# Weight subtractions and additions of a mixture-of-experts stage from GpSimd to VectorE, PSUM copies to ScalarE

## The chip, the cores and the metric

The kernel runs on one core of one Trainium2 chip. The metric is the device time of one execution in microseconds, as the median of several runs. TensorE multiplies, VectorE, ScalarE and GpSimd work on elements, SyncE's queue issues nearly all DMA transfers.

## The reference

Linear attention (random features) with a mixture of experts and a feed-forward behind it:

```python
q_p, k_p = (phi(q_s), phi(k_s))
...
x = np.ascontiguousarray(attn_out.transpose(0, 2, 1, 3)).reshape(B * S, H * D)
...
for e in range(E):            # E = 8, D = 512, F = 1024
    mask = expert_idx == e
    ...
    h = np.maximum(xe @ w1[e], 0.0)
    ye = h @ w2[e]
    out[mask] = gate_w[mask, None] * ye
...
h = x @ w_in                                            # 2304 x 512 times 512 x 2048
g = np.maximum(h, 0.0) + np.log1p(np.exp(-np.abs(h)))
return (g @ w_out).astype(np.float32)
```

The experts' weights are float32; w_in and w_out come as 64-bit floats.

## The kernel before

The program has three stages: attention with routing, the eight experts one after the other, and the feed-forward over 6 blocks of 384 tokens. Every product is made of three matmuls on operands that are split into a rounded part and a rest (`three`, L881 to L884), so each weight is first copied to a rounded form by ScalarE, and the rest is found by a subtraction.

An expert (`moe_expert`, L946) has 8 steps f. A step has 12 matmuls of the first layer into a bank "a", then ScalarE's relu hh (L957) and VectorE's rest hl (L958), and 12 matmuls of the second layer (`layer2`, L934) for the step two behind. Two banks hold "a", so TensorE comes back to the bank of step f, and to its hh and hl, only after the second layer's 12 matmuls, the next step's 12 and again 12 of the second layer.

Weights come through four buffers "raw" of 512 KB. `fetch_unit` (L251) issues the DMA on SyncE's queue; in the next step `split_unit` (L257) rounds the unit on ScalarE (L260) and subtracts (L263), on GpSimd for odd units and on VectorE for even ones. Each expert brings in 8 units, 64 in the stage, so 32 subtractions are on either engine. In every third step, until all 16 are done, half a block of w_in is fetched too, in the same buffers; `convert_w_in` (L229) makes a float32 of it with four VectorE instructions (`split_f64`, L193 to L199), an addition on GpSimd (L231), and a store to the scratch tensor wi_f, issued by SyncE (L232). From the last expert on, halves of w_out are split by `load_half` (L217: VectorE, ScalarE, and GpSimd at L222 and L223).

The next expert's x is gathered by GpSimd (L895), scaled by ScalarE (L906) and, part by part, transposed on TensorE (L913), rounded by ScalarE (L915) and its rest taken by VectorE (xl, L916). Behind an expert's last product `store_y` (L975) copies four PSUM banks to ys, two on VectorE (L981) and two on ScalarE (L983), and SyncE stores ys (L986) and the tokens' numbers (L989). `load_y` (L996) reads a block for the feed-forward, its rests by VectorE (L1005).

Each engine and SyncE's queue take their instructions in order; the order of the queues is planned when the program is built, from the program's order and a timeline of its own.

Of the kernel before, what the change touches and what calls it, by code (L numbers as in the profile page):

```python
# [15 lines left out]
AF = mybir.ActivationFunctionType  # L16
ALU = mybir.AluOpType
# [4 lines left out]
P = 128  # L22
# slots per expert: the first expert's, then the others' from the fullest to the emptiest
CAPS = (344, 344, 328, 312, 304, 292, 284, 264)
CAP = max(CAPS)
# [4 lines left out]
def tile_favor_moe_softplus(  # L30
# [42 lines left out]

    # a token's x and its gate
    x_tok = dram.tile([NT + P, DM + 1], F32, name="x_tok")
# [74 lines left out]
    def disjoint(ins, group):  # L150
        """Scatters of a group write rows of their own: none waits for another."""
        ins = getattr(ins, "ins", ins)
        tc.declare_no_dep(ins, group=group, reason="each token has a row of its own")
        tc.add_to_no_dep_group(group, ins)

    def behind(ins, other):
        """Of two instructions of an engine, the order."""
        if other is not None:
            tc.add_manual_dep(
                ins.ins, other.ins.name,  # L160
                mybir.DependencyInfo(mybir.DependencyClass.NoSync, mybir.DependencyReason.DATA),
                reason="keeps the engine's order")
# [3 lines left out]
    def expert_units(i, e):  # L166
        # the units of the expert at place i: expert e, a number or a register
        for j in range(4):
            a1 = w1[:, :, j * 256:(j + 1) * 256].rearrange("e (k p) f -> p e k f", p=P)
            a2 = w2[:, j * 256:(j + 1) * 256, :].rearrange("e (k p) f -> p e k f", p=P)  # L170
            units[8 * i + j] = a1[:, bass.ds(e, 1)].rearrange("p o k f -> p (o k) f")
            units[8 * i + 4 + j] = a2[:, bass.ds(e, 1)].rearrange("p o k f -> p (o k) f")
# [14 lines left out]
    def split_f64(raw, after):  # L187
        """64-bit floats as a float32 of their upper bits and a float32 of the rest."""
        hi, lo = raw[:, :, 1], raw[:, :, 0]
# [12 lines left out]

    # weights come a step or more before they are split: no engine waits for them

# [24 lines left out]
    def convert_w_in(j, hf, raw, after):  # L229
        a, _, r = split_f64(raw, after)  # L230
        nc.gpsimd.tensor_tensor(r, a, r, op=ALU.add)  # L231
        nc.sync.dma_start(units[8 * E + j][:, 2 * hf:2 * hf + 2, :],  # L232
                          r.rearrange("p (k f) -> p k f", k=2))
# [23 lines left out]
    def split_unit(i, raw, after):  # L257
        slot = ring[i % NRING]
        for c in range(0, 1024, 1024):
            ins = nc.scalar.activation(slot[:, c:c + 1024], raw[:, c:c + 1024], AF.Copy)  # L260
            if c == 0:
                behind(ins, after[0])
            (nc.gpsimd if i % 2 else nc.vector).tensor_tensor(  # L263
                slot[:, 1024 + c:1024 + c + 1024], raw[:, c:c + 1024],
# [4 lines left out]

# [1 line left out]
    pctx = ExitStack()  # L271
# [11 lines left out]
    with ExitStack() as actx:  # L283
# [5 lines left out]
        nc.gpsimd.memset(zero_w, 0.0)  # L289
        # NT: no token  # L290
        none_i = sm.tile([P, E * NT // P], I32, name="none_i", bufs=1)
# [7 lines left out]
        def clear_y():  # L299
            # rows that the first gather meets before their tokens' are written, or for no token  # L300
            nc.sync.dma_start(x_tok[NT:NT + P, :], zero_w)
# [9 lines left out]
            for c in range(KD):  # L311
                for j in range(0, NT, 512):
# [5 lines left out]
                       allow_small_or_imprecise_dtypes=True)  # L318
        # a token's number less NT, in two parts
        tok_hl = sm.tile([P, NTILE, 2], I32, name="tok_hl", bufs=1)  # L320
# [73 lines left out]

        # An item: the token tiles r, r+1 (or the mixed one) of a batch pair, of k or of q.
        class Item:
# [12 lines left out]
        xin, vin = {}, {}  # L409
        # the last items' tokens reach the first expert without a way through DRAM  # L410
        tail = items[-2:]
# [19 lines left out]
        def half_squares(it):  # L431
            it.sq = sm.tile([P, H, it.nr], F32, tag="sq", bufs=2, name="sq")
            step = 4 if it is items[0] else H
            for h in range(0, H, step):
                nc.vector.tensor_reduce(it.sq[:, h:h + step], it.x2[:, h:h + step], axis=AX.X,
                                        op=ALU.add)
            # sq cancels in (proj - sq) - (max - sq): (sq - ln(sqrt(M))) - sq
            up = sm.tile([P, H, it.nr], F32, tag="up", bufs=2, name="up")
# [7 lines left out]
        def transposes(it, g4):  # L446
# [8 lines left out]
            if it is items[1] and g4 == 0:  # L455
                behind(ins, first_done[0])
            # in a slot of the ring that is free so far
            k0 = DM * (1 + lows[0] % 3)
# [45 lines left out]

        # heads per bank; a head's two products with its neighbours' zeros overlap there
        GROUPS = ((0, 3), (3, 6), (6, 8))
# [25 lines left out]

        # kv per head: gate columns, z and kv of the first batch, then kv, z, gate of the second
        kvs = {}
# [30 lines left out]

        # where the 128 columns of a product start in kv, and where g, z and x are in a product;
        # the next product overwrites the columns that are not needed
        KV0 = (0, 2 * DG - P)
# [14 lines left out]
        def q_product(it, grp):  # L583
# [18 lines left out]
            def cols(g, lo, hi, c0, w):  # L602
                # [p, head, tile, w]: the columns c0, c0 + 1, ... of each product
                a = nm[lo:hi, c0:c0 + w]
# [25 lines left out]
        def route_pick(it):  # L630
# [17 lines left out]
            nc.vector.tensor_tensor(it.oh, cand, bc(cm), op=ALU.is_equal)  # L648
            # the one-hots before each tile of the item, summed
            it.ohs = sm.tile([P, 2, E], BF16, tag="ohsum", name="ohsum")  # L650
# [31 lines left out]
        def read_first():  # L682
            """The tokens of the first window so far."""
            nc.sync.dma_start(ids_0, id_slot[0:NC * P, :].rearrange("(c p) o -> p (c o)", p=P))

        def add_first(it, sl):
            """An item's tokens in the first window, by one-hots of their slots."""
            pid = ps.tile([P, NC, 2], F32, tag=TG, bufs=NTG, name="pid")
# [13 lines left out]
        def gather_first():  # L702
            """The rows of the first window, but for those of the last items."""
            for c in range(NC):
# [4 lines left out]
        def first_split():  # L709
            """The first window's x, transposed: gathered rows, and one-hots for the last items'."""  # L710
            xh, xl = (ring[i][:, 0:KD * NBLK].rearrange("p (k n) -> p k n", k=KD)
# [75 lines left out]
        NI = len(items)  # L787
        # the first expert's weights come when the second pair's k leaves time
        UNITS_AT = {10: (0, 1), 11: (2, 3), 12: (4, 5), 13: (6, 7)}
# [7 lines left out]
        for n in range(NI + 2):  # L797
# [47 lines left out]
            if n == NI - 2:  # L845
                # in the space of k and v
                a, b = (inp.tile([P, VO], F32, tag="kf", bufs=2, name="tail") for _ in range(2))
# [31 lines left out]

# [1 line left out]
    def three(o, wH, wL, xH, xL, first, last):  # L881
# [46 lines left out]

    # products of the second layer that are due, LAG steps behind the first layer's
    due = []  # L930
# [15 lines left out]
    def moe_expert(e, xh, xl, mid):  # L946
        n_e = CAPS[e]
        for f in range(NF):
# [17 lines left out]
            if f % 3 == 1 and to_convert:  # L966
                fetch_w_in(*to_convert.pop(0))
            # the first expert's x stays in the slots of units 11 and 15 until its last use
            for j in ((0, 4, 1, 5, 2, 6, 3, 7)[f:f + 1] if e or f < 6 else (3, 7) if f == 7 else ()):
# [5 lines left out]
    def store_y(e):  # L975
# [3 lines left out]
        for d in range(KD):  # L979
            if d % 2:  # L980
                nc.vector.tensor_copy(ys[:, d, 0:n_e], ops[d][:, 0:n_e])  # L981
            else:
                nc.scalar.activation(ys[:, d, 0:n_e], ops[d][:, 0:n_e], AF.Copy)  # L983
        reg = nc.sync.value_load(off_i[0:1, e:e + 1], min_val=max(0, NT - sum(CAPS[e:])),
# [25 lines left out]
    def places():  # L1010
        # tokens per expert; the experts behind the first by their tokens, the fullest first
        key = tb.tile([P, E], F32, tag="over", name="key")
# [21 lines left out]
        nc.vector.tensor_reduce(cntp[:, 1:E], more, axis=AX.X, op=ALU.add)  # L1034
        # where the places' windows start in the compact order
        off = tb.tile([P, E + 1], F32, tag="off", name="off")
# [13 lines left out]
    def windows():  # L1050
        # overflow windows: 128 slots each of the experts that hold more tokens than their slots
        over = tb.tile([P, E], F32, tag="over", name="over")
# [43 lines left out]

    # the parts of the next expert's x that are transposed in a step
    SPLIT_AT = {2: (0,), 3: (1,), 4: (2,), 5: (3,)}
# [29 lines left out]

# [1 line left out]
    def ff_layer1(a, f, yh, yl):  # L1130
# [54 lines left out]
    def ff_step(b, f, gh, gl):  # L1185
        if b == NB - 1 and f >= NF2 - 2:
            # the last two steps tile by tile: the first tiles leave while the last is computed
            ends.append((f, gh, gl))
# [34 lines left out]

# [1 line left out]
    n_over = nc.values_load(ntot[0:1, 0:1], min_val=0, max_val=NWIN)  # L1225
# [87 lines left out]
```

## Time and profile before

| what | us |
|---|---|
| median of 3 runs | 923.97 |
| shortest, longest run | 920.7, 926.7 |
| profiled execution, span from first to last instruction | 919.6 |

The page gives no time for the profiled execution beside its span; the shortest of the runs shown is 1.1 us above the span, the median 4.4. In the rows, a busy time is a sum over instructions in us, "mean" and the durations of a source view are in ns, and "idle before" is the time that the engine stood just before those instructions, with what ended it. PEclk is the granted TensorE clock as a share of full speed. A wait in SyncE's queue (SPq) delays all DMAs behind it.

### The profile page before, as it was taken

Reading aid. Unit: us, or ns where it says so; the run is one execution under the profiler, and the core shown is the slowest. Engines: PE = TensorE matmul, PEld = TensorE weight load, DVE = VectorE, ACT = ScalarE, POOL = GpSimd, SP = SyncE. Lnnn points to the kernel's source line nnn. Section 1 sums busy time; section 2 is a strip of 40 time slices with the busy share of each in tenths; the row PEclk is TensorE's granted clock in tenths of the full one; section 3 lists DMA queues with packets and bytes.
Section 4 is the critical chain, followed back from the end, with each engine's and each line's share of the span. In section 5 each row is a group of like instructions: output and inputs, shape, how many; then the busy total and the mean of one; then the engine's idle time right before and its main releaser. Section 6 shows DMA issues by size and latency. Waiting matters only on the chain.

```text
span 919.6 us, 14049 instructions
## 1 busy us (share of the span) xinstructions
PE 839.2 (91%) x5104; PEld 776.2 (84%) x5104; DVE 528.6 (57%) x1127; ACT 473.5 (51%) x1051; POOL 298.5 (32%) x290
## 2 busy tenths in 40 slices
PE   7798878995999899898997988999999999999996
PEld 6697778985899898798897976989898999999995
DVE  6489889985796685754688878323223323222221
ACT  4476658761544444444545545555545555445543
POOL 6454467422344544454355554100100100001001
PEclk9799998997989999998999999999999999999999
DMA  9992352024768668667675420101001000000001
GB/s 244 210 317 85 82 161 69 1 71 70 240 190 258 227 198 271 196 202 230 213 254 195 133 94 14 56 1 35 35 1 34 36 1 1 35 1 18 19 1 36
DMA packets 83308, 104.22 MB, mean 113 GB/s; under 512 B 16904, under 2 KB 62632, under 8 KB 83234
## 3 DMA queue, kind: packets, MB, share of 16 engines
q1 hardware_dynamic: 79442, 93.35, 33.8%
q0 software_dynamic: 3792, 9.92, 3.7%
q8 instruction: 42, 0.69, 0.4%
q14 instruction: 32, 0.26, 0.1%
HBM read 78.68 MB, written 24.58 MB: 112 GB/s over the span
## 4 chain that ended last, share of the span: by engine, by line
issue 40%; PE 19%; DVE 19%; DMA 12%; POOL 4%; ACT 3%; SPq 1%; POOLq 0%; DVEq 0%; ACTq 0%
DMA raw<-in_moe_w_dram 5%; DVE cva L193 2%; DVE w L263 2%; PE a L882 2%; PE a L884 2%; PE a L883 2%; DVE cva L196 2%; PE nm L593 2%; DVE mx L489 2%; POOL out_dram L1176 1%; DMA x_tok<-xt 1%; DMA vm<-in_v_dram 1%; ACT w L260 1%; DVE cvr L199 1%; PE y L882 1%
## 5 line engine op out<-in xcount | busy, mean ns | idle before, releaser
L1144 DVE SCALAR_TENSOR_TENSOR ab<-a,ab 128x384 f32<-128x384 f32 x96 | 53.4, 556 | 175.9 <-ACT ab L1143 167.2
L882 PE MATMUL a<-yh,w 128*128 128x384 f32 x384 | 131.0, 341 | 11.8 <-DVE ab L1144 11.8
L884 PE MATMUL a<-yh,w 128*128 128x384 f32 x384 | 130.2, 339 | 0.0
L883 PE MATMUL a<-yl,w 128*128 128x384 f32 x384 | 129.5, 337 | 0.0
L1176 POOL DMA_INDIRECT out_dram<-ob,idx x18 | 17.8, 989 | 323.9 <-ACT ob L1174 320.2
L1159 PE MATMUL o<-w,gh 128*128 128x512 f32 x288 | 114.7, 398 | 0.0
L1156 PE MATMUL o<-w,gh 128*128 128x512 f32 x288 | 114.0, 396 | 0.0
L1161 PE MATMUL o<-w,gl 128*128 128x512 f32 x288 | 113.7, 398 | 0.0
L1141 ACT ACTIVATE ab<-a 128x384 f32<-128x384 f32 x96 | 46.9, 489 | 107.9 <-PE a L884 107.8
L493 ACT ACTIVATE ph<-pj,nb 128x128 f32<-128x128 f32 x288 | 82.6, 393 | 31.6 <-DVE nb L491 22.3
L260 ACT ACTIVATE w<-raw 128x1024 fp32r<-128x1024 f32 x64 | 67.5, 1056 | 58.8 <-DMA raw<-in_moe_w_dram 53.4
L263 POOL TENSOR_TENSOR w<-raw,w 128x1024 fp32r<-128x1024 f32 x32 | 77.1, 2427 | 58.5 <-ACT w L260 58.4
L882 PEld LDWEIGHTS a<-yh,w 128*128 128x128 f32 x384 | 72.4, 189 | 19.3 <-DVE ab L1144 15.4
L1148 DVE TENSOR_TENSOR gl<-ab,gh 128x384 fp32r<-128x384 f32 x96 | 55.5, 578 | 50.5 <-ACT gh L1147 50.5
L882 PE MATMUL y<-hh,w 128*128 128x344 f32 (+6 forms) x256 | 79.1, 313 | 2.4 <-DVE ys L981 2.1
L1147 ACT ACTIVATE gh<-ab 128x384 fp32r<-128x384 f32 x96 | 50.4, 525 | 57.7 <-DVE ab L1144 57.7
L883 PE MATMUL y<-hl,w 128*128 128x344 f32 (+6 forms) x256 | 79.9, 313 | 0.0
L884 PE MATMUL y<-hh,w 128*128 128x344 f32 (+6 forms) x256 | 79.1, 311 | 0.0
L263 DVE TENSOR_TENSOR w<-raw,w 128x1024 fp32r<-128x1024 f32 x32 | 58.6, 1833 | 31.8 <-ACT w L260 31.7
L883 PEld LDWEIGHTS a<-yl,w 128*128 128x128 f32 x384 | 72.8, 189 | 3.9
L884 PEld LDWEIGHTS a<-yh,w 128*128 128x128 f32 x384 | 72.4, 189 | 0.0
L882 PE MATMUL a<-xh,w 128*128 128x344 f32 (+6 forms) x224 | 70.2, 313 | 2.0 <-DVE hl L958 2.0
(223 smaller groups left out, 2039.0 us busy)
## 6 DMA issues: line engine op xcount, KB each, us to landing
raw<-in_moe_w_dram SPq DMA_DIRECT2D x64, 512.0 KB
raw<-in_moe_w_in_dram SPq DMA_DIRECT2D x16, 512.0 KB
raw<-in_moe_w_out_dram SPq DMA_DIRECT2D x16, 512.0 KB
yb<-y_comp SPq DMA_DIRECT2D x6, 768.0 KB
x_tok<-xt SPq DMA_DIRECT2D x8, 513.0 KB
vf<-in_v_dram SPq DMA_DIRECT2D x4, 1024.0 KB
qf<-in_q_dram SPq DMA_DIRECT2D x4, 1024.0 KB
y_comp<-w SPq DMA_DIRECT2D x16, 256.0 KB
```

The costliest lines, as they stand in the source:

```text
L260: ins = nc.scalar.activation(slot[:, c:c + 1024], raw[:, c:c + 1024], AF.Copy)
L263: (nc.gpsimd if i % 2 else nc.vector).tensor_tensor(slot[:, 1024 + c:1024 + c + 1024], raw[:, c:c + 1024], slot[:, c:c + 1024].bitcast(F32 ...
L493: ins = nc.scalar.activation(dst[j], pj[:, j // 2, j % 2, :], AF.Exp, bias=nb[:, j // 2, j % 2:j % 2 + 1])
L882: nc.tensor.matmul(o, lhsT=wH, rhs=xH, start=first, stop=False)
L883: nc.tensor.matmul(o, lhsT=wH, rhs=xL, start=False, stop=False)
L884: nc.tensor.matmul(o, lhsT=wL, rhs=xH, start=False, stop=last)
L1144: nc.vector.scalar_tensor_tensor(ab, a, 0.0, ab, op0=ALU.max, op1=ALU.add)
L1147: placed[0] = nc.scalar.activation(gh, ab, AF.Copy)
L1148: placed[1] = nc.vector.tensor_tensor(gl, ab, gh.bitcast(F32), op=ALU.subtract)
L1156: ins = nc.tensor.matmul(os[t], lhsT=gh[:, s], rhs=u[:, c:c + DM], start=f == 0, stop=False)
L1159: nc.tensor.matmul(os[t], lhsT=gh[:, s], rhs=u[:, 1024 + c:1024 + c + DM], start=False, stop=False)
L1161: ins = nc.tensor.matmul(os[t], lhsT=gl[:, s], rhs=u[:, c:c + DM], start=False, stop=f == NF2 - 1)
```

## The change

The subtraction of every weight unit (L263) is on VectorE, for odd units too; the addition of w_in's two parts (L231) is on VectorE; all four copies of an expert's result out of PSUM are ScalarE's. GpSimd keeps the gathers and, for w_out, L222 and L223. The diff also takes comments out, which is left out here.

```diff
     def convert_w_in(j, hf, raw, after):
         a, _, r = split_f64(raw, after)
-        nc.gpsimd.tensor_tensor(r, a, r, op=ALU.add)
+        nc.vector.tensor_tensor(r, a, r, op=ALU.add)
         nc.sync.dma_start(units[8 * E + j][:, 2 * hf:2 * hf + 2, :],
                           r.rearrange("p (k f) -> p k f", k=2))
...
-            (nc.gpsimd if i % 2 else nc.vector).tensor_tensor(
+            nc.vector.tensor_tensor(
                 slot[:, 1024 + c:1024 + c + 1024], raw[:, c:c + 1024],
                 slot[:, c:c + 1024].bitcast(F32), op=ALU.subtract)
...
         for d in range(KD):
-            if d % 2:
-                nc.vector.tensor_copy(ys[:, d, 0:n_e], ops[d][:, 0:n_e])
-            else:
-                nc.scalar.activation(ys[:, d, 0:n_e], ops[d][:, 0:n_e], AF.Copy)
+            nc.scalar.activation(ys[:, d, 0:n_e], ops[d][:, 0:n_e], AF.Copy)
```

## Rows read from the trace of the kernel before

**Rows 1.** The page, its first part: busy us (share of the span) and instructions of each engine (VectorE is DVE, ScalarE ACT, GpSimd POOL).
```profile
PE 839.2 (91%) x5104; PEld 776.2 (84%) x5104; DVE 528.6 (57%) x1127; ACT 473.5 (51%) x1051; POOL 298.5 (32%) x290
```

**Rows 2.** Busy time by stretch: from and to, length, busy us (and instructions) of each engine, granted clock, DMA share, GB/s. The first three stretches are the experts', the fourth the feed-forward.
```profile
core 0: us, PE busy (x) PEld busy (x) DVE busy (x) ACT busy (x) POOL busy (x), PEclk, DMA share, GB/s
227.00:260.00 33.00, 29.74 (x172) 28.80 (x172) 27.73 (x83) 13.25 (x22) 10.26 (x7) 0.90 0.62 199
260.00:463.00 203.00, 188.82 (x1252) 181.85 (x1251) 131.90 (x175) 93.59 (x157) 96.17 (x57) 0.97 0.73 225
463.00:503.00 40.00, 35.08 (x244) 33.74 (x242) 34.60 (x41) 18.15 (x34) 21.50 (x11) 0.96 0.68 227
...
560.00:919.00 359.00, 346.46 (x1716) 311.13 (x1715) 111.17 (x194) 181.90 (x358) 24.50 (x23) 0.99 0.06 21
```

**Rows 3.** What TensorE's matmuls waited for between 227 and 503 us: who waited, for whom, us in total, times, longest.
```profile
PE xtp L913 <- DVE xl L916: 12.9, 7, 3.1
PE a L882 <- DVE hl L958: 3.6, 4, 1.6
PE a L882 <- DVE ab L1144: 3.5, 1, 3.5
PE y L882 <- DVE ys L981: 2.1, 2, 1.6
```

**Rows 4.** Costs by line between 227 and 503 us, on VectorE and (the last) ScalarE: count | busy us, mean ns | idle time before, with what ended it.
```profile
L263 DVE TENSOR_TENSOR w<-raw,w 128x1024 fp32r<-128x1024 f32 x32 | 58.6, 1833 | 31.8 <-ACT w L260 31.7
...
L193 DVE TENSOR_SCALAR cva<-raw 128x512 int32<-128x512 int32 x20 | 24.3, 1214 | 8.2 <-DMA raw<-in_moe_w_in_dram 6.6 <-DMA raw<-in_moe_w_out_dram 1.6
L196 DVE SCALAR_TENSOR_TENSOR cva<-raw,cva 128x512 int32<-128x512 int32 x20 | 18.7, 937 | 0.5
L199 DVE SCALAR_TENSOR_TENSOR cvr<-raw,cvs 128x512 f32<-128x512 uint32 x19 | 15.5, 816 | 4.5 <-DMA wi_f<-cvr 4.2
...
L981 DVE COPY ys<-y 128x344 f32<-128x344 f32 (+6 forms) x16 | 7.5, 468 | 0.0
...
L983 ACT ACTIVATE ys<-y 128x344 f32<-128x344 f32 (+6 forms) x16 | 5.9, 423 | 0.0
```

**Rows 5.** The same lines one by one, over the whole span: count, shortest/median/longest duration in ns, first and last start.
```profile
L263 DVE TENSOR_TENSOR w<-raw,w x32: 1207/1226/6276, 237.3 to 487.3; 128x1024 fp32r<-128x1024 f32 x32
L263 POOL TENSOR_TENSOR w<-raw,w x32: 2358/2408/2765, 243.8 to 499.8; 128x1024 fp32r<-128x1024 f32 x32
...
L231 POOL TENSOR_TENSOR cvr<-cva,cvr x16: 1272/1286/1318, 246.2 to 417.8; 128x512 f32<-128x512 f32 x16
...
L193 DVE TENSOR_SCALAR cva<-raw x32: 406/427/5561, 238.5 to 564.6; 128x512 int32<-128x512 int32 x32
...
L196 DVE SCALAR_TENSOR_TENSOR cva<-raw,cva x32: 679/693/2762, 239.3 to 565.0; 128x512 int32<-128x512 int32 x32
...
L199 DVE SCALAR_TENSOR_TENSOR cvr<-raw,cvs x32: 676/693/2717, 241.6 to 567.5; 128x512 f32<-128x512 uint32 x32
```

**Rows 6.** Time line of VectorE and GpSimd at 299 to 307 us: start us, us, engine, line and operation.
```profile
299.49 4.79 POOL L263 TENSOR_TENSOR w<-raw,w 128x1024 fp32r<-128x1024 f32 x2
304.21 1.31 POOL L231 TENSOR_TENSOR cvr<-cva,cvr 128x512 f32<-128x512 f32 x1
...
300.34 6.28 DVE L263 TENSOR_TENSOR w<-raw,w 128x1024 fp32r<-128x1024 f32 x1
306.54 0.50 DVE L981 COPY ys<-y 128x344 f32<-128x344 f32 x1
```

**Rows 7.** Time line of ScalarE, SyncE's queue and TensorE in the same expert, up to 317 us; in brackets the idle time before, and what ended it.
```profile
300.20 0.80 ACT L983 ACTIVATE ys<-y 128x344 f32<-128x344 f32 x2
...
305.55 0.37 SPq L232 DMA_DIRECT2D wi_f<-cvr  x1
307.17 0.39 SPq L986 DMA_DIRECT2D y_comp<-ys  x1
...
308.79 1.80 SPq L254 DMA_DIRECT2D raw<-in_moe_w_dram  x3
...
314.04 1.06 ACT L260 ACTIVATE w<-raw 128x1024 fp32r<-128x1024 f32 x1 [7.40 <-DMA raw<-in_moe_w_dram]
...
316.80 0.63 PE L913 MATMUL xtp<-ident,xg 128*128 128x128 f32 x3 [3.14 <-DVE xl L916]
```

**Rows 8.** One stretch of 5 us behind it, columns as in rows 2.
```profile
320.00:325.00 5.00, 5.00 (x29) 4.76 (x29) 4.97 (x7) 2.16 (x4) 1.47 (x1) 0.86 0.75 222
```

**Rows 9.** What SyncE's queue waited for between 227 and 503 us, columns as in rows 3.
```profile
SPq L183 <- POOL w L263: 32.8, 4, 10.5
SPq L254 <- POOL w L263: 32.5, 16, 3.3
SPq L986 <- DVE ys L981: 22.2, 6, 14.2
SPq L232 <- POOL cvr L231: 20.3, 11, 5.6
```

**Rows 10.** What GpSimd, VectorE and ScalarE waited for in the same stretch, from three views, columns as in rows 3.
```profile
POOL w L263 <- ACT w L260: 58.4, 12, 11.4
...
DVE w L263 <- ACT w L260: 31.7, 13, 6.5
...
ACT w L260 <- DMA raw<-in_moe_w_dram: 53.4, 22, 7.4
```

## The prediction

> **What bounds the kernel now.** I read the page first for the load of the engines: GpSimd is busy a third of the span and VectorE 57% [rows 1], so on the face of it the change puts work from an idle engine on a fuller one. A share of busy time is an average over stages, so next I read the busy time by stage. Experts run from about 227 to 503 us, and only there does the change act; the stretch behind it is listed for comparison [rows 2]. In the expert stretches TensorE is busy 29.74 + 188.82 + 35.08 = 253.6 of 276 us, and its granted clock is 0.90, 0.97 and 0.96, which means that in part of them it stood at 1.2 instead of 2.4 GHz. So TensorE is what the stage is made of, and there are two things to win: its 22.4 us of idle time, and the clock, 0.10 x 33 + 0.03 x 203 + 0.04 x 40 = 11.0 us, of which some falls on the idle time itself. I put the clock's share at 9 us: the most that this change can give back is some 31 us.
>
> Third, who ends TensorE's idle time: VectorE, nearly always. 12.9 us are transposes of the next expert's x that wait for xl, 3.6 us wait for hl, 2.1 us for ys, and 3.5 us is the first softplus of the feed-forward [rows 3]. Why is VectorE late with 57% of load? The costs by line and the shortest, median and longest duration of the same lines answer it. The subtraction of L263 takes 1833 ns on average on VectorE but 1226 ns in the median, and up to 6276; L193 takes 1214 against 427, with a longest of 5561 [rows 4, 5]. An instruction with a fixed shape that takes five or thirteen times its median is not computing. The time line shows what it does: the L263 on VectorE that begins at 300.34 runs 6.28 us, to 306.62. GpSimd ran two L263 and one L231 back to back from 299.49 to 305.52 [rows 6]. 305.52 plus 1.1 is the end of VectorE's instruction: it stood until GpSimd was through, then took its usual time.
>
> Fourth, how this reaches TensorE, since hl and xl have slack. In the same expert: the second ys copy on VectorE stands behind that L263 (306.54). SyncE issues DMAs in order; its store of wi_f follows GpSimd's add (305.55), the store of ys follows the copy (307.17), and three fetches of weights come only behind them, at 308.79. They share the DMA engines, ScalarE has its first at 314.04 after 7.40 us of idle time, behind that stands the rest of its queue, and TensorE goes on at 316.80 after 3.14 us [rows 7]. The clock then reads 0.86 for 320 to 325 [rows 8]. Over all experts SyncE's queue waits 32.8 + 32.5 us for GpSimd's L263 (to free a buffer of raw weights), 20.3 us for its add and 22.2 us for VectorE's ys copy [rows 9]: all four are what the change touches.
>
> **The change part by part.** *Subtractions:* 32 L263 leave GpSimd, 2408 ns each, and come to VectorE at 1226, so +39.2 us there [rows 5]. *Additions:* 16 of L231, 1286 ns on GpSimd. VectorE has no such addition in the trace; the nearest rows are L199, 128x512 with two inputs, median 693 ns, and half an L263, 613 ns. I take 693: +11.1 us (bounds 9.8 and 11.1) [rows 5]. *Copies:* 16 of L981 leave VectorE, -7.5 us, and ScalarE gets 16 more at the 423 ns of L983, +6.8 us [rows 4]. *Stalls:* if GpSimd has no tensor work in the stage, the excess over the medians goes: L263 58.6 - 32 x 1.226 = 19.4, L193 24.3 - 20 x 0.427 = 15.8, L196 18.7 - 20 x 0.693 = 4.8, L199 15.5 - 19 x 0.693 = 2.3, together 42.3 us [rows 4, 5]. VectorE's busy time in the stage is 27.73 + 131.90 + 34.60 = 194.2 us now [rows 2], and after 194.2 + 39.2 + 11.1 - 7.5 - 42.3 = 194.7 us. It does all of the work in the time in which it now does part of it and stands. Bounds: 237 us if no stall goes, still under 276.
>
> ScalarE is busy 13.25 + 93.59 + 18.15 = 125.0 of 276 us [rows 2]; 6.8 more are hidden beside TensorE as long as the four copies end before the next expert's second layer wants their banks. Four in a row are 4 x 0.42 = 1.7 us [rows 4]. In the expert looked at, ScalarE's two begin at 300.20, and VectorE's second only at 306.54, behind the stalled L263 [rows 6, 7]. The store waits for all four, so here it could leave at about 302 to 303, not at 307.17. The Trainium skill, page "TensorEngine Tiling (Array Packing)", section "PSUM Bottleneck", says to use both ScalarE and VectorE for PSUM evacuation; by it the copies on one engine would be exposed and cost half of 1.7 us in each of 8 experts, 7 us, and the sum below would end 7 us higher. I follow the row, since there the second engine was the late one.
>
> *What the path gains, expert by expert.* In the expert of rows 7, VectorE has behind 300.34 its own L263, the two of GpSimd and the addition, 3 x 1.226 + 0.693 = 4.4 us, unstalled: 304.7 at the latest for the store of wi_f, and its turn in SyncE's queue comes 2.4 us or more ahead of 307.17. The gap to close there is 3.14 us. The seven waits for xl average 12.9 / 7 = 1.8 us and the ys waits 1.0, so an earlier fetch of 2.4 us covers most of them [rows 3]. I take 0.8 of the xl, hl and ys waits of the stage, 0.8 x (12.9 + 3.6 + 2.1) = 14.9 us, and half of the clock's 9 us, 4.5, since the clock falls only behind such gaps but not all of them go. The 3.5 us at the first softplus I leave: the splits of w_out on GpSimd (L222, L223) are not part of the change, and VectorE gets more subtractions there. Together -19.4 us; against it I set 1.4 us for new short waits behind the longer VectorE queue, about one L263. So the profile's span goes from 919.6 to about 901.6. The runs' median, 923.97, stands 4.4 us over that span, and I keep this distance: **906 us**, with 897 to 915 as the own range of this case.
>
> What is queued behind the added work: on VectorE, behind a subtraction that waits for ScalarE's L260, stand hl and xl. hl has slack. TensorE runs three blocks of 12 matmuls before it needs that bank or product, 36 x 188.82 / 1252 = 5.4 us [rows 2]. One to three L263 and an addition (1.2 to 4.4 us) fit into it. On GpSimd only the gathers of the next x are left, which now wait for nothing but their own inputs; on SyncE the wi_f store waits for VectorE's addition, right behind L199.
>
> **The rivals.** *The fetch stays late.* DMA engines are busy 0.73 of the time between 260 and 463 us, and ScalarE's L260 waits 53.4 us for raw weights [rows 2, 10]. If these come from the bursts, with four buffers, and not from SyncE's waits, the xl gaps stay, and only hl and ys go with a little clock: 3.6 + 2.1 = 5.7 us, 918 us. For it: three fetches at once took 5.25 us from issue to use [rows 7]. Against it: at 0.73 the DMA engines stand a quarter of that time, and 65 us of SyncE's waits name GpSimd [rows 9]. Chance 0.19.
>
> *VectorE becomes the blocker, and it is slower.* GpSimd's L263 waited 58.4 us in 12 waits for ScalarE's L260; VectorE's own waited 31.7 us in 13 [rows 10]. VectorE runs in order, so all of those waits can now hold up hl and xl. Both engines mostly waited for the same late fetch; but if the difference, 58.4 - 31.7 = 26.7 us, is added to VectorE, and the stalls that go, worth 14.9 us on the path, are taken off, it comes to +12 us: 936 us. It decides where one wait and the subtractions behind it exceed the 5.4 us of slack; the longest wait of GpSimd was 11.4 us [rows 10], so it can. Each queue's order is fixed when the program is built, so a late fetch can't be stepped around. The Trainium skill, page "Perfetto Trace Analysis", section "Optimizing Scalar/DVE Operations", has a rule against the change: where VectorE is saturated, work should go to ScalarE or even GpSimd; it adds that a move between VectorE and GpSimd might not help, as they share a port. By its first half the time would be this rival's, by the second it would not. Chance 0.12.
>
> *The copies on ScalarE are exposed*, 906 + 7 = 913 us: for it, that ScalarE stands up to 7.4 us for raw weights with the copies possibly behind it; against it, that half of them stood there already. Chance 0.06.
>
> *More is won*: all of the 31 us but the first softplus, 27 us, 897 us or below. Chance 0.08. The forecast itself has 0.55.
>
> **How the numbers follow.** 906 is the forecast's. 1% is 9.2 us, about what a measurement of this kernel can tell from no change, as three runs spread over 6 us; the bounds are 914.7 and 933.2. Faster: 0.55 less its upper edge, plus 0.08 and most of 0.06, gives 0.66. Same: the late fetch, the edges and the mild part of the slower rival, 0.24. Slower: 0.10. The range takes the forecast, the exposed copies and the late fetch, 893 to 926; above it lies the slower rival, below it little.
>
> **What would show it.** After the change VectorE's L263 and L193 should have means near their medians, 1.23 and 0.43 us, outside the last expert, with VectorE's busy time in the stage near 195 us. SyncE's waits should name GpSimd no more in the first seven experts, the ys store should leave 2 to 5 us sooner behind the last product, and TensorE's waits for xl should fall from 12.9 us to some 3, with the clock at 0.98 or more between 260 and the end of the seventh expert. I am wrong if ScalarE's waits for raw weights stay at 53 us, or if hl waits on VectorE for TensorE's account grow past 3.6 us because subtractions stand in front of it.

## The result, and the profile after

| | median us | runs | span of the profiled run |
|---|---|---|---|
| before, with a fourth run | 922.34 | 4, 918.29 to 926.7 | 919.6 |
| changed | 882.18 | 4, 879.91 to 884.77 | 878.1 |

The changed kernel takes 0.9611 of the time of the kernel before, 95% interval 0.9574 to 0.9648: some 40 us faster, where 18 had been forecast, and below the range's 893.

The busy time by stretch of the changed kernel, columns as in [rows 2]; the experts end near 458 us now:
```profile
222.00:260.00 38.00, 37.64 (x242) 37.10 (x241) 33.26 (x103) 19.40 (x33) 6.80 (x6) 1.00 0.74 236
260.00:450.00 190.00, 190.00 (x1341) 185.40 (x1340) 135.30 (x207) 103.17 (x178) 20.73 (x18) 1.00 0.81 256
450.00:490.00 40.00, 38.79 (x204) 33.83 (x202) 33.17 (x50) 23.61 (x49) 20.99 (x14) 1.00 0.56 173
```
TensorE has no idle time left between 260 and 450 us and its granted clock is 1.00 throughout, where it was 0.97 [rows 2]. VectorE is busy 33.26 + 135.30 = 168.6 of the first 228 us, 0.74, where it was 194.2 of 276, 0.70 [rows 2]: with more work, hardly fuller. The DMA share went up, from 0.73 to 0.81: the same bytes in less time.

What TensorE's matmuls waited for between 222 and 500 us, against [rows 3]:
```profile
PE a L882 <- DVE ab L1141: 2.0, 3, 1.1
PE y L882 <- ACT hh L957: 0.4, 1, 0.4
PE o L1158 <- DVE gl L1145: 0.2, 1, 0.2
```
The waits for xl, hl and ys, 18.6 us before, are gone, not reduced.

Costs by line in the same stretch, then L263 one by one, against [rows 4, 5] (lines behind L980 have moved up by three):
```profile
L263 DVE TENSOR_TENSOR w<-raw,w 128x1024 fp32r<-128x1024 f32 x64 | 78.0, 1219 | 27.3 <-ACT w L260 27.1
...
L196 DVE SCALAR_TENSOR_TENSOR cva<-raw,cva 128x512 int32<-128x512 int32 x27 | 25.1, 928 | 0.7
...
L193 DVE TENSOR_SCALAR cva<-raw 128x512 int32<-128x512 int32 x27 | 12.6, 467 | 6.6 <-POOL cvs L222 6.5
...
L980 ACT ACTIVATE ys<-y 128x344 f32<-128x344 f32 (+6 forms) x32 | 11.2, 434 | 0.0
L231 DVE TENSOR_TENSOR cvr<-cva,cvr 128x512 f32<-128x512 f32 x16 | 10.9, 683 | 0.1
...
L263 DVE TENSOR_TENSOR w<-raw,w x64: 1209/1218/1227, 230.8 to 461.7; 128x1024 fp32r<-128x1024 f32 x64
```
All 64 subtractions take 1209 to 1227 ns; before, half as many took from 1207 to 6276. L196 still has a mean of 928 ns: the stretch holds the start of the feed-forward, where GpSimd does L222 and L223.

The place of [rows 6, 7], the second step of the third expert, in the time lines of ScalarE, SyncE's queue and TensorE after the change:
```profile
287.65 1.49 ACT L980 ACTIVATE ys<-y 128x344 f32<-128x344 f32 x4
...
296.10 1.06 ACT L260 ACTIVATE w<-raw 128x1024 fp32r<-128x1024 f32 x1 [2.10 <-DMA raw<-in_moe_w_dram]
...
288.16 0.37 SPq L232 DMA_DIRECT2D wi_f<-cvr  x1
289.17 0.40 SPq L983 DMA_DIRECT2D y_comp<-ys  x1
...
290.79 1.75 SPq L254 DMA_DIRECT2D raw<-in_moe_w_dram  x3
...
300.42 0.58 PE L913 MATMUL xtp<-ident,xg 128*128 128x128 f32 x3
```
From ScalarE's first copy to the store of ys it is 289.17 - 287.65 = 1.5 us now, and was 307.17 - 300.20 = 7.0. The three fetches follow 3.1 us behind that copy, where they followed 8.6 us behind it: 5.5 us sooner. ScalarE waits 2.10 us for the first of them, not 7.40, and the third part's transposes (300.42), which had stood 3.14 us until 316.80 [rows 7], follow without a wait.

Where the 40 us lie is read from two starts: ScalarE's first relu (L957), with which the experts begin, and VectorE's first softplus (L1144, after the change L1141), with which the feed-forward does. Source view: durations in ns, then the first and last start; before, then after:
```profile
L957 ACT ACTIVATE hh<-a x64: 372/428/460, 230.4 to 486.0; 128x344 fp32r<-128x344 f32 x16, 128x328 fp32r<-128x328 f32 x8, 128x312 fp32r<-128x312 f32 x8, 128x304 fp32r<-128x304 f32 x8
...
L1144 DVE SCALAR_TENSOR_TENSOR ab<-a,ab x96: 543/558/559, 496.7 to 906.1; 128x384 f32<-128x384 f32 x96
```
```profile
L957 ACT ACTIVATE hh<-a x64: 373/429/462, 224.3 to 449.7; 128x344 fp32r<-128x344 f32 x16, 128x328 fp32r<-128x328 f32 x8, 128x312 fp32r<-128x312 f32 x8, 128x304 fp32r<-128x304 f32 x8
...
L1141 DVE SCALAR_TENSOR_TENSOR ab<-a,ab x96: 541/558/559, 457.6 to 864.7; 128x384 f32<-128x384 f32 x96
```
The experts went from 496.7 - 230.4 = 266.3 to 457.6 - 224.3 = 233.3 us, 33.0 less. The feed-forward went from 919.6 - 496.7 = 422.9 to 420.5. The remaining 6.1 us are the attention in front of the experts. Its TensorE instructions are the same in the same order, and in the runs below the experts begin at 219.4 to 225.8 us, also in those that hold only a small part of the change: the 6.1 us are a difference between two executions, not work of the change. The medians and differences of medians below leave out runs more than 1.5% above the fastest of their kernel. On the three chips of the experiments the kernel before takes 909.56 to 914.47 us; the changed kernel, run again on one of them, takes 881.47.

### The profile page after: what moved, and what is told of

The parts are those of the page before. It is cut to its first block, busy times and chain, and to the rows that moved or that the text cites. A ratio compares the mean times of both kernels' runs of the same rounds, so it can differ in the third digit from the quotient of the medians.

```text
span 878.1 us, 14005 instructions
## 1 busy us (share of the span) xinstructions
PE 825.8 (94%) x5104; PEld 764.6 (87%) x5104; DVE 515.8 (59%) x1159; ACT 479.0 (55%) x1067; POOL 204.6 (23%) x242
## 5 line engine op out<-in xcount | busy, mean ns | idle before, releaser
L1141 DVE SCALAR_TENSOR_TENSOR ab<-a,ab 128x384 f32<-128x384 f32 x96 | 53.3, 556 | 174.4 <-ACT ab L1140 174.2
L493 ACT ACTIVATE ph<-pj,nb 128x128 f32<-128x128 f32 x288 | 82.8, 394 | 30.9 <-DVE nb L491 21.3
L263 DVE TENSOR_TENSOR w<-raw,w 128x1024 fp32r<-128x1024 f32 x64 | 78.0, 1219 | 27.3 <-ACT w L260 27.1
L260 ACT ACTIVATE w<-raw 128x1024 fp32r<-128x1024 f32 x64 | 67.5, 1057 | 29.0 <-DMA raw<-in_moe_w_dram 25.8
L1144 ACT ACTIVATE gh<-ab 128x384 fp32r<-128x384 f32 x96 | 50.4, 525 | 56.7 <-DVE ab L1141 56.5
L884 PE MATMUL y<-hh,w 128*128 128x344 f32 (+6 forms) x256 | 78.3, 306 | 0.0
L882 PE MATMUL y<-hh,w 128*128 128x344 f32 (+6 forms) x256 | 77.0, 305 | 0.4 <-ACT hh L957 0.4
L883 PE MATMUL a<-xl,w 128*128 128x344 f32 (+6 forms) x224 | 67.7, 302 | 0.0
```

Of the source, the lines that this page charges most:

```text
L263: nc.vector.tensor_tensor(slot[:, 1024 + c:1024 + c + 1024], raw[:, c:c + 1024], slot[:, c:c + 1024].bitcast(F32), op=ALU.subtract)
L493: ins = nc.scalar.activation(dst[j], pj[:, j // 2, j % 2, :], AF.Exp, bias=nb[:, j // 2, j % 2:j % 2 + 1])
L882: nc.tensor.matmul(o, lhsT=wH, rhs=xH, start=first, stop=False)
L883: nc.tensor.matmul(o, lhsT=wH, rhs=xL, start=False, stop=False)
L884: nc.tensor.matmul(o, lhsT=wL, rhs=xH, start=False, stop=last)
L1141: nc.vector.scalar_tensor_tensor(ab, a, 0.0, ab, op0=ALU.max, op1=ALU.add)
```

## The experiments

Two explanations were set against each other. **Theory A**: VectorE stands while GpSimd reads SBUF, and the gain is these stalls. **Theory B**: GpSimd's results come late (its subtraction takes 2408 ns, VectorE's 1226 [rows 5]), so raw buffers, the wi_f store and the ys store hold SyncE's queue, whatever stalls VectorE. "Experts" is the stretch from the first relu to the first softplus, as above, from each run's profile; the ratio is to the kernel before on the same chip. e1 to e4 ran on one chip, e5 to e8 on a second, e9 to e12 on a third.

| run | median us | ratio, 95% interval | experts, us |
|---|---|---|---|
| only subtractions (e1_subs) | 881.04 | 0.9645, 0.9582 to 0.9708 | 234.2 |
| only additions (e2_adds) | 909.89 | 0.9958, 0.9916 to 1.0001 | 258.8 |
| only copies (e3_copies) | 904.61 | 0.9886, 0.9803 to 0.9969 | 256.1 |
| changed, copies shared (e4_no_copies) | 879.84 | 0.9639, 0.9575 to 0.9704 | 233.0 |
| changed, 3 raw buffers (e7_three_raw) | 900.22 | 0.9895, 0.9848 to 0.9942 | 254.5 |
| the same + GpSimd reads (e5_idle_reads) | 915.34 | 1.0017, 0.9964 to 1.0069 | 261.8 |
| the same + GpSimd writes (e6_idle_writes) | 899.17 | 0.9876, 0.9852 to 0.9901 | 251.8 |
| changed + w_out on VectorE (e8_wout) | 869.94 | 0.9558, 0.9537 to 0.9580 | 234.1 |
| changed, again (e9_after_again) | 881.47 | 0.9694, 0.9596 to 0.9791 | 234.0 |
| changed + GpSimd reads (e10_reads_4raw) | 900.03 | 0.9908, 0.9860 to 0.9956 | 251.4 |
| changed + late release (e11_late_release) | 890.38 | 0.9790, 0.9677 to 0.9904 | 243.1 |
| changed + later release (e12_later_release) | 897.66 | 0.9878, 0.9774 to 0.9983 | 251.5 |

### One part at a time

The kernel before with only the subtractions moved:
```diff
-            (nc.gpsimd if i % 2 else nc.vector).tensor_tensor(
+            nc.vector.tensor_tensor(
```


> Only the 32 odd subtractions go to VectorE; additions stay on GpSimd, copies stay shared. Theory A (VectorE stands while GpSimd reads; the gain is in the stalls): GpSimd's tensor work in the expert stage falls from 97.7 to 20.6 us, so about four fifths of the 40 us come back: 30 to 36 us faster than before, 887 to 893. Theory B (SyncE's queue is what matters: the shared ys copies and the addition hold it up, whatever stalls VectorE): without those two parts half of it at most, 15 to 20 us faster.

33.4 us faster than before on that chip, and the experts take 234.2 us against 233.3 of the full change. The subtractions alone are sufficient; theory B's "half at most" falls. The run does not tell stalls from raw buffers, since both go with the subtractions. But the additions on GpSimd still stall VectorE in it:
```profile
L263 DVE TENSOR_TENSOR w<-raw,w 128x1024 fp32r<-128x1024 f32 x64 | 86.8, 1356 | 30.9 <-ACT w L260 30.4
```
That is 8.8 us more than the 78.0 us of the changed kernel, and the experts take no longer: a stall that fits into the slack costs nothing.

Only the addition moved:
```diff
-        nc.gpsimd.tensor_tensor(r, a, r, op=ALU.add)
+        nc.vector.tensor_tensor(r, a, r, op=ALU.add)
```


> Only the 16 additions for w_in go to VectorE. Theory A: a fifth of GpSimd's tensor time goes, 5 to 9 us faster. Theory B: SyncE waits 20.3 us for the addition; with it on VectorE, but behind stalled instructions, 8 to 12 us faster. If VectorE's extra load matters more than either, no change or slower.

4.6 us by the medians, with an interval that just reaches 1. The experts are 7.5 us shorter in the profile, as theory A had it, but against one profile of before that proves little.

Only the copies on ScalarE:
```diff
-            if d % 2:
-                nc.vector.tensor_copy(ys[:, d, 0:n_e], ops[d][:, 0:n_e])
-            else:
-                nc.scalar.activation(ys[:, d, 0:n_e], ops[d][:, 0:n_e], AF.Copy)
+            nc.scalar.activation(ys[:, d, 0:n_e], ops[d][:, 0:n_e], AF.Copy)
```


> Only the copies out of PSUM go to ScalarE alone. Theory A: VectorE's stalls stay, the ys store leaves 2 to 5 us sooner but the fetches behind it still wait for GpSimd: 0 to 6 us faster. Theory B: the ys store is the one that holds up the fetches (22.2 us of SyncE's waits): 10 to 15 us faster. By the rule that both engines should empty PSUM: up to 7 us slower.

9.9 us by the medians, and 10.2 in the experts against the first profile of before. The interval, some 3 to 18 us, reaches into the ranges of both theories. While VectorE is stalled, a ys store that does not depend on it is worth something.

The changed kernel with the copies shared again (the last diff, reversed):

> The changed kernel with the copies shared between VectorE and ScalarE again. Theory A: within 3 us of the changed kernel, 880 to 886. Theory B: 8 to 12 us of the gain are lost, 890 to 895.

879.84 against 881.04 for the subtractions alone and 881.47 for the full change: no difference. The parts are not additive. The copies are worth some 10 us beside stalls and nothing without them. ScalarE alone costs nothing either: the Trainium skill, page "TensorEngine Tiling (Array Packing)", section "PSUM Bottleneck", asks for both engines to empty PSUM, and here 32 copies of 434 ns by ScalarE alone were no slower than the shared ones.

### GpSimd work for which nobody waits

One raw buffer less made room for a scratch tile, so this kernel is first the base of the next two:
```diff
-    more_stg = ctx.enter_context(tc.tile_pool(name="more_stg", bufs=1))
-    stages = itertools.cycle((stg, stg, stg) + 1 * (more_stg,))
+    stages = itertools.cycle((stg, stg, stg))
```


> The changed kernel with three buffers for raw weights in place of four; it is also the base of the next two. If buffers that come free sooner carry the gain (theory B), one buffer less gives back much of it: 900 or more. If the gain is VectorE's stalls (theory A), the fetches keep slack: 882 to 888.

900.22 us, what theory B expected. The changed kernel did not run on this chip; its 881.47 on another is 18.8 less, and its experts take 234.0 us against 254.5. Its lines on VectorE and ScalarE in the expert stage:
```profile
L263 DVE TENSOR_TENSOR w<-raw,w 128x1024 fp32r<-128x1024 f32 x64 | 78.2, 1222 | 44.2 <-ACT w L260 44.2
L260 ACT ACTIVATE w<-raw 128x1024 fp32r<-128x1024 f32 x64 | 67.8, 1059 | 88.8 <-DMA raw<-in_moe_w_dram 77.9 <-DMA raw<-wi_f 10.5
```
No subtraction is stalled, and yet ScalarE waits 88.8 us for weights. So four buffers leave little to spare at this pace, and a buffer that comes free late can matter.

On this base, 32 subtractions on GpSimd that nothing reads, behind the L260 of each odd unit:
```diff
+            if i % 2:
+                nc.gpsimd.tensor_tensor(idle, idle, slot[:, c:c + 1024].bitcast(F32),
+                                        op=ALU.subtract)
```


> Three buffers, and GpSimd does 32 subtractions of the former shape and at their former place (behind ScalarE's rounding of each odd unit), on a scratch tile that nothing reads: work that only takes GpSimd and the memory's ports. Theory A: VectorE's stalls come back with it, L263 on VectorE to a mean of 1.7 us or more, and 20 to 30 us of the gain are lost against the base with three buffers. Theory B (slow results of GpSimd were what others waited for): nobody waits for these, so within 3 us of the base.

15 us are lost against the base by the medians. The six runs spread from 906.15 to 916.97 us, and the profiled one, with 7.3 us lost in the experts, is one of the two fastest. In the same place, GpSimd only writes (two fills for each odd unit, started behind the same L260):
```diff
+            if i % 2:
+                for _ in range(2):
+                    idler = nc.gpsimd.memset(idle, 0.0)
...
```


> As the one before, but GpSimd writes zeros (two fills of 128x1024 for each odd unit) and reads nothing. If any GpSimd work stalls VectorE, the loss is that of the reading kernel, scaled by its busy time. If only two readers collide, VectorE's subtractions stay at 1.23 us; the one-input instructions (L193, L198) may still stall, so at most a third of the reading kernel's loss.

899.17 us, nothing lost. Lines of the reading kernel, then of the writing one:
```profile
L263 DVE TENSOR_TENSOR w<-raw,w 128x1024 fp32r<-128x1024 f32 x64 | 107.0, 1671 | 23.7 <-ACT w L260 22.7 <-issue 0.9
L267 POOL TENSOR_TENSOR idle<-idle,w 128x1024 f32<-128x1024 f32 x32 | 93.7, 2930 | 102.6 <-ACT w L260 101.7
```
```profile
L263 DVE TENSOR_TENSOR w<-raw,w 128x1024 fp32r<-128x1024 f32 x64 | 78.2, 1222 | 39.9 <-ACT w L260 39.5
...
L268 POOL MEMSET idle<- 128x1024 f32 x64 | 61.4, 960 | 119.3 <-ACT w L260 117.2
```
VectorE's subtractions go from 1222 to 1671 ns beside GpSimd's reading, and stay at 1222 beside 61 us of its writing. For L263, with two inputs in SBUF, the stall is a collision of readers. L193 has one input, and it does stand beside fills, if little; these are its lines up to 430 us, ahead of GpSimd's work for w_out, of the base and of the writing kernel:
```profile
L193 DVE TENSOR_SCALAR cva<-raw 128x512 int32<-128x512 int32 x16 | 6.8, 424 | 10.2 <-DMA raw<-in_moe_w_in_dram 10.1
```
```profile
L193 DVE TENSOR_SCALAR cva<-raw 128x512 int32<-128x512 int32 x16 | 7.8, 489 | 7.8 <-DMA raw<-in_moe_w_in_dram 7.8
```
The loss beside the reading is smaller than the 20 to 30 us of theory A. The base already stood for its fetches: L263's waits for L260 fell from 44.2 to 22.7 us as its busy time grew, so part of the stall fell into time in which VectorE waited anyway.

### Stall and late release apart, with four buffers

GpSimd reads as many elements as its former subtraction did, holds no raw buffer, and writes to a tile that the feed-forward uses later:
```diff
+            if i % 2:
+                for c0, c1 in ((0, 384), (384, 768), (768, 1024)):
+                    idle = mm.tile([P, NBLK], F32, tag="ab", name="idle")
+                    nc.gpsimd.tensor_tensor(idle[:, 0:c1 - c0], slot[:, c0:c1].bitcast(F32),
+                                            slot[:, c0:c1].bitcast(F32), op=ALU.subtract)
```


> The changed kernel with all four raw buffers, and GpSimd reads the same number of elements as in its former subtraction, behind ScalarE's rounding of each odd unit, in three pieces; it writes scratch that nothing reads, and holds no raw buffer. Theory A (VectorE's stalls carry the gain): 15 to 30 us are lost against the changed kernel. Theory B (the raw buffers that GpSimd held longer carry it): under 5 us are lost.

The changed kernel itself ran beside it, with the expectation:

> The changed kernel once more, so that the runs beside it have it on the same chip: 0.961 of the kernel before by the first measurement, 0.965 if a part of that was the attention, in which nothing differs and which took 6 us longer in the profile of before.

It came to 0.9694; the interval, 0.9596 to 0.9791, holds both numbers. By the medians it is 909.56 - 881.47 = 28.1 us faster than before on this chip.

18.6 us are lost against the changed kernel on the same chip (900.03 to 881.47), 17.4 of them in the experts. Two lines of the reading kernel, and what its TensorE waited for:
```profile
L269 POOL TENSOR_TENSOR idle<-w 128x384 f32<-128x384 f32 (+1 forms) x96 | 103.3, 1108 | 65.4 <-ACT w L260 64.7 <-DVE gl L1150 0.5
L263 DVE TENSOR_TENSOR w<-raw,w 128x1024 fp32r<-128x1024 f32 x64 | 92.9, 1452 | 23.0 <-ACT w L260 23.0
```
```profile
PE a L887 <- DVE ab L1146: 5.7, 2, 4.4
PE a L887 <- DVE hl L963: 5.1, 3, 3.0
PE xtp L918 <- DVE xl L921: 2.6, 4, 1.1
```
L263 is at 1452 ns, and hl and xl are late again, though nobody waits for GpSimd's results. The dose is not that of the kernel before: the three pieces take GpSimd 103.3 us, more than the 77.1 us of its former 32 subtractions, while L263's mean of 1452 ns stays below the 1833 of [rows 4]. So 18.6 us shows that stalls alone cost time, and not what share they had.

The other half: a fill of the used raw buffer, so that only its release is later.
```diff
+            if i % 2:
+                nc.gpsimd.memset(raw, 0.0)
```


> The changed kernel, and GpSimd fills the raw buffer of each odd unit with zeros once it has been used, 0.96 us of writing without any reading: the buffer comes free about as late as behind GpSimd's former subtraction (1.2 + 1.0 against 2.4 us), but VectorE's two-input instructions don't collide with it. Theory A: under 4 us are lost. Theory B: 12 to 25 us are lost.

890.38 us, 8.9 lost, between the two expectations. The intervals of the ratios overlap with those of the changed kernel, but the runs don't (886.26 to 894.47 against 878.77 to 882.08). Lines of the kernel, and two of its SyncE waits:
```profile
L263 DVE TENSOR_TENSOR w<-raw,w 128x1024 fp32r<-128x1024 f32 x64 | 80.4, 1256 | 31.7 <-ACT w L260 31.6
...
L267 POOL MEMSET raw<- 128x1024 f32 x32 | 31.2, 986 | 117.9 <-DVE w L263 90.8 <-DMA raw<-in_moe_w_dram 14.0 <-DMA raw<-in_moe_w_in_dram 12.8
```
```profile
SPq L183 <- POOL raw L267: 45.3, 8, 10.1
SPq L254 <- POOL raw L267: 30.4, 15, 4.0
```
The subtractions are all but unstalled, and SyncE's queue waits for GpSimd as it did in [rows 9]. The release is not quite alone: up to 430 us L193 and L198, with one input each, take 2.5 us more beside the fills than in the changed kernel. With three fills in a loop instead of one:

> The same with three fills, so that the odd units' buffers come free 2.9 us later. Theory B: the loss grows with the delay, to 25 us or more. Theory A: still under 6 us; how much delay the fetches bear without loss is then read here.

897.66 us, 16.2 lost: it grows with the delay, if less than theory B wanted. A part of it is again VectorE beside fills, as L193 shows up to 430 us (424 ns in the line of the base above):
```profile
L193 DVE TENSOR_SCALAR cva<-raw 128x512 int32<-128x512 int32 x16 | 10.1, 630 | 22.0 <-DMA raw<-in_moe_w_in_dram 22.0
```

### A version that beats both

The two GpSimd instructions for w_out go to VectorE as well:
```diff
-        nc.gpsimd.tensor_tensor(d, a, wh.bitcast(F32), op=ALU.subtract)
-        nc.gpsimd.tensor_tensor(slot[:, 1024 + hf * 512:1024 + (hf + 1) * 512], d, r, op=ALU.add)
+        nc.vector.tensor_tensor(d, a, wh.bitcast(F32), op=ALU.subtract)
+        nc.vector.tensor_tensor(slot[:, 1024 + hf * 512:1024 + (hf + 1) * 512], d, r, op=ALU.add)
```


> The changed kernel with the subtraction and addition for w_out (L222, L223) on VectorE too, so that GpSimd has no tensor work behind the attention. Theory A: the stalls between 440 and 520 us go as well, against some 22 us more VectorE work in the first feed-forward block: 0 to 8 us faster than the changed kernel. If VectorE is full there, up to 5 us slower.

869.94 us, 0.9558 of the kernel before, and more than was expected: 11.5 us below the changed kernel, though on another chip. The experts are as before that step, 234.1 us; the feed-forward takes 409.5 us in its profile against 420.5, and the gain is in its first block. The stretch from 490 to 540 us, of the changed kernel and then of this one, columns as in [rows 2]:
```profile
490.00:540.00 50.00, 43.19 (x206) 36.18 (x206) 38.62 (x56) 26.86 (x56) 25.36 (x18) 1.00 0.20 64
```
```profile
490.00:540.00 50.00, 50.00 (x253) 45.21 (x252) 38.28 (x72) 30.16 (x62) 3.04 (x3) 1.00 0.20 68
```
VectorE gets through 72 instructions in the 38.28 us in which it got through 56, and TensorE is never idle.

## Why the prediction was right in its mechanism and wrong in its size

**The stall** was read rightly. VectorE's L263 went from a mean of 1833 to 1219 ns, and the addition took 683 ns where 693 was assumed. Its load did not grow, 185.58 us before and 172.94 after between the first relu and the first softplus (lines below), and TensorE lost nothing to it. That L263 is stalled by GpSimd's *readers* and not by its fills is shown by e5 and e6; the Trainium skill, page "SBUF — State Buffer", section "Who interferes with whom", states it: the port pair that the two engines share is an exclusive lock, and a VectorE instruction with two SBUF inputs contends with a GpSimd instruction that reads SBUF, not with one that only writes it. The runs agree, 1671 against 1222 ns. hl, which has one input in PSUM, fits it too: 476 ns on average in the changed kernel run again, 471 beside GpSimd's reading in e10. That sentence does not cover L193, whose 15.8 us were the second largest part of the 42.3 us of stalls that the text added up: with one input it stood up to 5561 ns [rows 5], and it also stands beside fills (e6, e12).

**The way to TensorE** was right: the ys store leaves 5.5 us sooner, the fetch with it, and xl is not late. SyncE's waits no longer name GpSimd, as the text had looked for, but those for ys and the addition did not shrink: 21.3 and 19.6 us after the change, as these two rows of the changed kernel show against [rows 9]:
```profile
SPq L983 <- ACT ys L980: 21.3, 6, 11.9
...
SPq L232 <- DVE cvr L231: 19.6, 7, 5.9
```
These are waits for work that is not due yet. Their sum says nothing of lateness; the distance from the last product to the store does.

**The step that failed** is "I take 0.8 of the xl, hl and ys waits of the stage, ... and half of the clock's 9 us", with the first softplus left out and 1.4 us set against it. It came to 18 us, and the experts gave 33.0. From the first relu to the first softplus, before and then after, columns as in [rows 2]:
```profile
230.40:496.70 266.30, 244.56 (x1621) 236.14 (x1620) 185.58 (x272) 121.82 (x204) 122.66 (x72) 0.96 0.72 224
```
```profile
224.30:457.60 233.30, 232.94 (x1620) 227.90 (x1619) 172.94 (x306) 127.29 (x218) 31.52 (x26) 1.00 0.80 253
```
TensorE's idle time fell from 21.7 to 0.4 us, by 21.4. The other 11.6 us are the clock: the same matmuls are busy 232.94 us at 1.00 where they were 244.56 at 0.96. So the term most too small was the clock's, 4.5 us against 11.6. The waits for xl, hl and ys gave all 18.6 us, not 14.9; the other 2.8 us of idle time are for the most part the wait for the first softplus, which the text had put at nothing; and the 1.4 us of new waits did not come. The first part of the text held the true size: 22.4 us of idle time and 11.0 of clock, of which it counted 9, some 31 us as the most that could be won.

What the discount got wrong is how a gap behaves. It is what is left of a lateness when the slack is used up: 3.14 us in the expert looked at, where the fetch came 5.5 us sooner. In the five other experts in which transposes wait for xl behind a ys store, that store leaves 3.0 to 5.3 us sooner behind ScalarE's first copy, and the wait had been 0.45 to 2.68 us. The advance was the larger in each, so these gaps closed whole. In slices of 5 us of this stage the clock before was under 1.00 only at and behind gaps, so it went to 1.00 with them. A factor of 0.8 suits a cost that is spread evenly, not a threshold. The text had worked out "2.4 us or more" of advance and took it as 2.4; in that expert it was more than twice as much. Late release, for which the text had named 65 us of SyncE's waits, had no term of its own in the sum.

The size itself differs between measurements. Of the 41.5 us between the two profiles, 6.1 are the attention, which is not the change's; by the medians the two kernels stood 28.1 us apart on the chip of e9, and on that of e1 and e4 the kernel before stood 33.4 and 34.6 us above those two.

**The rivals.** "The fetch stays late" did not come to pass, but its mechanism is close at hand: with three buffers some 19 us are lost. ScalarE's wait for raw weights fell from 53.4 [rows 10] to 25.8 us in the changed kernel. "VectorE becomes the blocker" is refuted. "The copies on ScalarE are exposed" is too: they can be shared or not, 879.84 and 881.47. "More is won", given 0.08, was the one that came true.

**What stays open.** Stall alone costs 18.6 us (e10) and late release, all but alone, 8.9 (e11). That they add up to 27.5 of the 28.1 us between the two kernels on that chip proves no split: both experiments differ from the old kernel in dose, 103 us of reading against 77 and a release set by one fill, the second has some stall in it, and e1 kept 8.8 us of stalls at no cost. What share each had in the kernel before is not shown.

## What to carry to other kernels

Where one line has a mean far above its median on VectorE, look at what GpSimd does in those microseconds before moving work to the idle engine: the same work on VectorE alone can be free. When a change makes a chain earlier, compare its advance with the longest gap, stage by stage: where it was more, as here, the gaps went whole and the clock behind them came back too, and not a fraction. And parts of such a change don't add up: the one that removes the common cause takes the gain of the others.

## What the runs showed of the hardware that was not expected

Three GpSimd instructions one behind the other kept one VectorE subtraction waiting through all three, 6.28 us [rows 6]; VectorE did not get in between. The collision costs both sides: GpSimd's subtraction of 128x1024 took 2930 ns on average in e5, with a shortest of 2386, where its former ones had a median of 2408 [rows 5]. And 61 us of GpSimd fills in e6 left VectorE's two-input subtractions at 1222 ns, while the one-input L193 went from 424 to 489 ns beside them, and to 630 beside three fills in a row (e12).
